# Experts in float16 halves, with the first layer's units on the partitions

## The chip, the cores and the metric

One core of a Trainium2 chip. The metric is device time in microseconds (us) of one launch; "the span" is the time from the first to the last instruction in the profile, and the device time of the same execution is 1.8 us longer.

## The reference

Hashed attention over 4 batches of 8 heads (768 tokens, 64 numbers a head), then a mixture layer with one expert per batch, applied to the 128 tokens of the batch with the highest gate scores:

```python
mask = q_bucket[:, :, :, None] == k_bucket[:, :, None, :]
scores = np.where(mask, scale * np.matmul(q, k.transpose(0, 1, 3, 2)), -1e9)
attn = softmax(scores)                      # max, exp, sum
x = attn @ v                                # heads side by side: 512 numbers a token
...
scores = np.einsum('bsd,d->bs', x, w_gate)
for b in range(B):
    top_idx = np.argpartition(-scores[b], capacity)[:capacity]
    xe = x[b, top_idx]                      # 128 x 512
    h = np.maximum(xe @ w1, 0.0)            # 128 x 1024
    ye = h @ w2                             # 128 x 512
    g = 1.0 / (1.0 + np.exp(-scores[b, top_idx]))
    out[b, top_idx] = x[b, top_idx] + g[:, None] * ye
```

## The kernel before

The 32 heads follow each other as a software pipeline. For each head a maximum phase (products mx, L340) runs some 14 units ahead of its score products (st, L385 and L389), the exponentials on ScalarE (L403, L405), the subtraction R on VectorE or GpSimd (L418), which gives the low half of the exponentials, and the attention products (av, L442). Where a number has to be kept to float32, it is held as a high and a low half and the product is made of three products.

The order of all this is written out by hand: every step has a time in units (nine to a head) worked out from the table T, a heap hands the steps out in order of time, and each engine gets its instructions in that order and keeps it. The token choice and the expert of a batch are generators in the same heap: what a generator yields is how many units later it goes on. `load_w` splits the two weight matrices into halves in the first 11 heads or so: a copy on ScalarE (L508) and a subtraction on GpSimd (L510), 16 of each.

Batch 0's expert is applied by `apply_expert` after the choice of batch 0, between heads 12 and 15. Batch 1's expert runs late, after batch 2's choice (the first `yield` below), mixed into heads 28 to 31 (heads are counted from 0); when it ends, batch 2's begins, no earlier than the second `yield` says:

```python
        if b == 2:
            yield -(9 * (NH - 2) + T["m1"])
            for y in apply_expert(1):
                yield y * T["y1"]
            yield -(9 * NH + T["m2"])
            st["fast"] = apply_expert_fast(2, LATE, mo_bank, mx_bank)
            yield from st["fast"]
```

A negative yield is an absolute time (here 253.1 and 279.3), and the choice and pause ahead of expert 1 end at 258.2, so that it starts there. Batch 3's part is the end of the kernel: `rank_last` takes the last scores (a product, a sum and two small steps on VectorE, after the last reciprocal L454 and its six copies on ScalarE L467), spreads them over the partitions by TensorE (bp, L851), compares on VectorE (L528 to L536), counts on TensorE (L540), finds the indices (idx, L882) and gathers the 128 rows (xe, L606). Then whatever expert 2 has not yet issued is issued, then eight products that only keep TensorE at work (wp, L894), then expert 3 (`apply_expert_last`).

An expert goes so: four transposes (xp, L628), three halves of xe (L635 to L637), the first layer of 24 products of 512 columns in two halves (mh, L662), a relu (L668), eight transposes (ht, L674), three halves of h (L686, L687, L692), the second layer of 24 products of 512 columns (yp, L700), the gate (L644 to L654), one step on VectorE that adds the result to the row (ye, L707) and a scatter by GpSimd's queue (L708).

Of the kernel before, what the change touches and what calls it, by code (L numbers as in the profile page):

```python
# [21 lines left out]
P = 128  # L22
# [9 lines left out]
VS = 16.0  # L32
DS = 2.0 ** -60
# [7 lines left out]
XHB = 2  # L41
# [10 lines left out]
    f2=2.4, l0=2.78, l1=6.42, l2=0.65, l3=5.3, lw=0.16, lw1=4.2, lw2=3.2, po=7.32,  # L52
# [30 lines left out]
def body(ctx, tc, qk, v, pj, wg, w1, w2, cst, out):  # L83
# [68 lines left out]
    w1h = cp.tile([P, 4, FF], F32R, name="w1h")  # L152
    w1l = cp.tile([P, 4, FF], BF16, name="w1l")
    w2h = cp.tile([P, 8, DM], F32R, name="w2h")
# [339 lines left out]
    def load_w(i):  # L494
# [11 lines left out]
        for e in range(2):  # L506
            sl = slice(e * 512, e * 512 + 512)
            nc.scalar.copy(hi[:, sl], t[:, sl])  # L508
            yield 1
            turn(nc.gpsimd.tensor_tensor(  # L510
                lo[:, sl], t[:, sl], hi[:, sl].bitcast(F32), op=ALU.subtract
            ))
            yield T["lw2"]
# [98 lines left out]
    def expert(b, tags):  # L612
# [19 lines left out]
        def split_x():  # L632
            xp = t["xp"]
            xh, xl, xb = tile_("xth", 512, F32R), tile_("xtl", 512, F32R), tile_("xtb", 512, BF16)
            nc.scalar.copy(xh, xp)  # L635
            nc.vector.tensor_tensor(xl, xp, xh.bitcast(F32), op=ALU.subtract)
            nc.scalar.copy(xb, xh.bitcast(F32))  # L637
            t["x"] = ((xh, w1h), (xl, w1h), (xb, w1l))
            t["hs"] = tile_("hs", FF, F32)
# [11 lines left out]
        def gate2():  # L651
            ss = t["ss"]
            nc.vector.tensor_scalar(ss[:, 1:2], ss[:, 1:2], 1.0, None, op0=ALU.add)
            nc.vector.reciprocal(ss[:, 1:2], ss[:, 1:2])  # L654

        def up(hp, e, ks, order=(0, 1, 2), by_part=False):
            ki = [(k, i) for k in ks for i in order]
            if by_part:
                ki = [(k, i) for i in order for k in ks]
            for k, i in ki:  # L660
                l, r = t["x"][i]
                nc.tensor.matmul(  # L662
                    hp, l[:, k * P : (k + 1) * P], r[:, k, e * 512 : e * 512 + 512],
                    start=(k == 0 and i == order[0]), stop=(k == 3 and i == order[-1]),
                )

        def relu(hp, e):
            nc.scalar.activation(t["hs"][:, e * 512 : e * 512 + 512], hp, AF.Relu)  # L668

        def turn_h(tp, e):  # L670
            t["tp", e] = tp
            for k in range(4):
                o = e * 512 + k * P
                nc.tensor.transpose(  # L674
                    out=tp[:, k * P : (k + 1) * P], in_=t["hs"][:, o : o + P], identity=ident
                )

        def split_h(e):
            if e == 0:
                t["h"] = [  # L680
                    (tile_("hth", FF, F32R), w2h), (tile_("htl", FF, F32R), w2h),
                    (tile_("htb", FF, BF16), w2l),
                ]
            (hh, _), (hl, _), (hb, _) = t["h"]
            f, tp = slice(e * 512, e * 512 + 512), t["tp", e]
            nc.scalar.copy(hh[:, f], tp)  # L686
            nc.scalar.copy(hb[:, f], hh[:, f].bitcast(F32))  # L687

        def split_h2(e):
            (hh, _), (hl, _), _ = t["h"]  # L690
            f, tp = slice(e * 512, e * 512 + 512), t["tp", e]
            nc.vector.tensor_tensor(hl[:, f], tp, hh[:, f].bitcast(F32), op=ALU.subtract)  # L692
# [20 lines left out]
        for f in (turn_x, split_x, gate, gate2, up, relu, turn_h, split_h, split_h2, down, finish):  # L713
# [4 lines left out]
        xth=("M3", 1), xtl=("M2x", 1), xtb=("M2", 2), hs=("M0", 1), hth=("M1", 1),  # L718
        htl=("M2x", 1), htb=("M3", 1), ye=("jk", 1),
    )  # L720
    LATE = dict(MAIN, htl=("X", XB), htb=("V", 1), ye=("X", XB))
    LAST = dict(
        xth=("XH", XHB), xtl=("XL", XLB), xtb=("R", 6), hs=("P", 4), hth=("P", 4),
        htl=("P", 4), htb=("P", 4), ye=("X", XB),
# [11 lines left out]
    def apply_expert(b):  # L736
# [9 lines left out]
        for e in range(2):  # L746
            hp = mo_bank(f"mh{b}_{e}")
            for k in range(4):
                m.up(hp, e, (k,))
                yield 1  # L750
            m.relu(hp, e)
            yield 2
        for e in range(2):
            m.turn_h(mo_bank(f"ht{b}_{e}"), e)
            yield 1
            m.split_h(e)
            yield 0.5
            m.split_h2(e)
            yield 1.5
# [7 lines left out]
    def apply_expert_fast(b, tags, bank, bank2):  # L767
# [7 lines left out]
        for k in range(4):  # L775
            m.up(h0, 0, (k,))
            yield T["f1"]
        m.relu(h0, 0)
        h1 = bank2(f"mh{b}_1")
        for k in range(2):  # L780
            m.up(h1, 1, (k,))
            yield T["f1"]
        m.gate2()
        m.turn_h(bank(f"ht{b}_0"), 0)
        m.split_h(0)
        yield T["f2"]
        m.split_h2(0)
        for k in range(2, 4):
            m.up(h1, 1, (k,))
            yield T["f1"]  # L790
        m.relu(h1, 1)
        yp = bank2(f"yp{b}")
        for k in range(2):
            m.down(yp, (k,))
            yield T["f1"]
        m.turn_h(bank(f"ht{b}_1"), 1)
        m.split_h(1)
        yield T["f2"]
        m.split_h2(1)
        for k in range(2, 8):  # L800
# [4 lines left out]
    def apply_expert_last(b, tags, bank, bank2):  # L805
# [6 lines left out]
        m.up(h0, 0, range(4), (0, 2, 1), True)  # L812
        m.relu(h0, 0)
# [238 lines left out]
```

## Time and profile before

| | |
|---|---|
| time, median of 3 runs (lowest to highest) | 487.26 us (485.84 to 487.91) |
| the profiled execution: time, span | 488.31 us, 486.5 us |
| mean granted TensorE clock | 0.956 |
| TensorE matmul busy | 430.6 us (89% of the span) |
| VectorE busy | 396.5 us (81%) |
| ScalarE busy | 344.0 us (71%) |
| GpSimd busy | 171.7 us (35%) |

The shares are means over stages that have different limits. The busy time of products is modelled and they overlap in the pipeline: one row's time is longer than the distance to the next, and what a product costs in a stream is the distance between starts.

### The profile page before, as it was taken

How to read it: one execution, taken by the hardware profiler on the slowest of the kernel's cores; microseconds unless marked ns; L12 is line 12 of the kernel's file. 1: busy time of each engine (PE TensorE's matmuls, PEld its weight loads, DVE VectorE, ACT ScalarE, POOL GpSimd, SP SyncE). 2: the span in 40 equal slices, each digit the busy share in tenths (PEclk: the TensorE clock that was granted, in tenths of full speed). 3: DMA queues.
4: the chain of work that ended last, by engine and by line, in shares of the span. 5: the costliest groups of instructions: out<-in, count | busy, mean ns of one | idle time of the engine just before them, and what ended most of it. 6: DMA issues, size and time to landing. Idle time of an engine off the chain costs nothing. (4 is left out here: it accounts for less than half of the span.)

```text
span 486.5 us, 14126 instructions
## 1 busy us (share of the span) xinstructions
PE 430.6 (89%) x5379; PEld 283.9 (58%) x5393; DVE 396.5 (81%) x991; ACT 344.0 (71%) x826; POOL 171.7 (35%) x137
## 2 busy tenths in 40 slices
PE   4789999978997898999998889899897899998795
PEld 3146666555654665676656566566565666666463
DVE  5669989999999997777799999999999977656611
ACT  2588898889885876787777579698775778763312
POOL 7025654445463352222413242324242333232300
PEclk9689999999999798999999899999998889999999
DMA  4774535545663233342464226445531133102010
GB/s 127 235 200 131 168 100 169 179 123 136 197 190 96 81 112 98 120 111 67 143 186 123 77 66 169 140 127 137 157 111 44 30 106 98 34 2 88 2 43 22
DMA packets 36167, 55.30 MB, mean 114 GB/s; under 512 B 6194, under 2 KB 27396, under 8 KB 36100
## 3 DMA queue, kind: packets, MB, share of 16 engines
q1 hardware_dynamic: 24676, 34.85, 26.2%
q10 hardware_dynamic: 10592, 17.44, 11.4%
q0 software_dynamic: 832, 2.11, 1.4%
q8 instruction: 42, 0.69, 0.6%
q14 instruction: 25, 0.20, 0.1%
HBM read 25.78 MB, written 7.35 MB: 68 GB/s over the span
## 5 line engine op out<-in xcount | busy, mean ns | idle before, releaser
L418 POOL TENSOR_TENSOR R<-P 128x768 f16<-128x768 f32 x80 | 124.9, 1562 | 246.9 <-DVE xd L334 95.1
L403 ACT ACTIVATE P<-st 128x512 f32<-128x512 f32 x192 | 113.2, 608 | 37.1 <-PE st L389 35.2
L442 PEld LDWEIGHTS <-P 128*128 128x128 bf16 x2304 | 120.1, 99 | 30.2 <-issue 20.3
L442 PE MATMUL av<-V,P 128*128 128x65 f16 (+1 forms) x2304 | 128.0, 196 | 0.0
L442 PE MATMUL av<-V,R 128*128 128x65 f16 x1152 | 123.1, 194 | 3.9 <-POOL R L418 2.3
L418 DVE TENSOR_TENSOR R<-P 128x768 f16<-128x768 f32 x112 | 119.5, 1067 | 7.0 <-ACT P L405 6.8
L385 PE MATMUL st<-A 97*128 97x256 f16 (+1 forms) x384 | 123.4, 333 | 0.3
L389 PE MATMUL st<-B 128*128 128x256 f16 (+1 forms) x384 | 123.3, 333 | 0.0
L356 DVE CUSTOM_DVE_ANT_0 mj<-mx,me 128x384 bf16<-128x384 f32 x192 | 106.2, 553 | 20.8 <-PE mx L340 8.4
L348 ACT ACTIVATE me<-mx 128x384 f32<-128x384 f32 x192 | 95.3, 497 | 28.7 <-DVE m L356 14.0
L442 PEld LDWEIGHTS <-R 128*128 128x128 f16 x1152 | 108.5, 100 | 5.2 <-POOL R L418 2.7
L340 PE MATMUL mx<-K,A 96*128 96x384 f16 x192 | 60.7, 344 | 10.4 <-DVE oneb L159 4.7
L405 ACT ACTIVATE P<-st 128x512 f32<-128x512 f32 x96 | 58.0, 604 | 11.3 <-PE st L389 10.0
L340 PE MATMUL mx<-A 96*128 96x384 f16 x192 | 64.6, 338 | 1.4 <-ACT me L348 0.7
L340 PEld LDWEIGHTS <-A 96*128 96x128 f16 x384 | 36.3, 100 | 30.0 <-issue 12.2
L467 ACT ACTIVATE x<-av,rc 128x64 f32<-128x64 f32 x192 | 42.2, 311 | 12.1 <-DVE rc L454 11.9
L385 PEld LDWEIGHTS <-A 97*128 97x128 f16 x384 | 38.1, 99 | 21.2 <-issue 7.2
L389 PEld LDWEIGHTS <-B 128*128 128x128 f16 x384 | 38.3, 100 | 18.7 <-issue 1.9
L235 DVE SCALAR_TENSOR_TENSOR XL<-X,XH 128x768 f16<-128x768 f32 x32 | 39.7, 1242 | 2.3 <-DMA B<-XL 2.3
L230 ACT ACTIVATE XH<-X 128x768 f16<-128x768 f32 x32 | 27.1, 850 | 7.6 <-DMA X<-in_qk_dram 7.6
L203 PE MATMUL hp<-X,pjt 128*32 128x384 f32 x128 | 17.6, 524 | 1.9 <-DMA X<-in_qk_dram 1.8
L334 DVE TENSOR_TENSOR xd<-XH 64x384 f16<-64x384 f16 x32 | 12.7, 397 | 8.0 <-ACT XH L230 7.1
(115 smaller groups left out, 498.4 us busy)
## 6 DMA issues: line engine op xcount, KB each, us to landing
X<-in_qk_dram SPq DMA_DIRECT2D x31, 384.0 KB
V<-in_v_dram ACTq DMA_DIRECT2D x16, 384.0 KB
A<-XH SPq DMA_DIRECT2D x64, 96.0 KB
B<-A SPq DMA_DIRECT2D x64, 96.0 KB
B<-XL SPq DMA_DIRECT2D x64, 96.0 KB
out_dram<-x ACTq DMA_DIRECT2D x8, 768.0 KB
W<-in_w_dram ACTq DMA_DIRECT2D x8, 512.0 KB
K<-xd SPq DMA_DIRECT2D x32, 48.0 KB
```

Source lines behind the costliest of these rows:

```text
L230: nc.scalar.activation(xh, st["X", h], AF.Copy, scale=XS)
L235: mine(nc.vector.scalar_tensor_tensor(xl, st["X", h], XS, st["XH", h], op0=ALU.mult, op1=ALU.subtract))
L340: nc.tensor.matmul(pt[:, :384], a[0:96, 0, t * P : (t + 1) * P], a[0:96, 1, 384:768] if i else K[h % NA][0:96], start=True, stop=True,)
L348: nc.scalar.activation(me, st["mx", h, t, 0][:, :384], AF.Relu)
L356: nc.vector.tensor_tensor_reduce(out=jk, in0=st["mx", h, t, 1][:, :384], in1=st["me", h, t], op0=ALU.add, op1=ALU.max, scale=1.0 / MS, sca ...
L385: nc.tensor.matmul(pt[:, o : o + n], a[:, 1, c * P : (c + 1) * P], a[:, 0, q0 : q0 + n], start=True, stop=False,)
L389: nc.tensor.matmul(pt[:, o : o + n], bt[:, 1, c * P : (c + 1) * P], bt[:, 0, q0 : q0 + n], start=False, stop=True,)
L403: nc.scalar.activation(pp[:, r, 0:512], pt, AF.Exp, scale=ES)
L405: nc.scalar.activation(pp[:, :, 512:768], pt.rearrange("p (a b) -> p a b", a=2), AF.Exp, scale=ES)
L418: (turn if pool else mine)(eng.tensor_tensor(t, pp[:, r, :], hi_view(pp, r), op=ALU.subtract))
L442: nc.tensor.matmul(o[:, t, 0:n], l, vv[:, c, hh, v0 : v0 + n], start=False, stop=last and l is lo, skip_group_check=True,)
L467: nc.scalar.activation(x[:, t], o[:, t, 0:D], AF.Copy, scale=rc[:, t : t + 1])
```

## The change

The high halves w1h and w2h, xth and hth become float16, and so do the low halves of x and h (the weights' low halves stay bfloat16). x is scaled by 16 on the way in, and the gate takes the 16 out again. The float16 high half serves in the third product too, so that the bfloat16 copies xtb and htb go. The first layer is turned round: the weights are the stationary operand and x the moving one, in 96 products of 128 columns instead of 24 of 512, so that the hidden units come out on the partitions. The second layer wants them there, and the transposes ht and the copy hs go; relu and split are made straight from the first layer's result, by ScalarE (high half) and VectorE (low half). The table T stays as it is, but for the entry f2, the two waits for a transpose in `apply_expert_fast`; the generators yield less in all, so that steps behind them get earlier times. The tiles that the halves use move to other tags.

```diff
-    w1h = cp.tile([P, 4, FF], F32R, name="w1h")
+    w1h = cp.tile([P, 4, FF], F16, name="w1h")
     w1l = cp.tile([P, 4, FF], BF16, name="w1l")
-    w2h = cp.tile([P, 8, DM], F32R, name="w2h")
+    w2h = cp.tile([P, 8, DM], F16, name="w2h")
...
             turn(nc.gpsimd.tensor_tensor(
-                lo[:, sl], t[:, sl], hi[:, sl].bitcast(F32), op=ALU.subtract
+                lo[:, sl], t[:, sl], hi[:, sl], op=ALU.subtract
             ))
...
-            xh, xl, xb = tile_("xth", 512, F32R), tile_("xtl", 512, F32R), tile_("xtb", 512, BF16)
-            nc.scalar.copy(xh, xp)
-            nc.vector.tensor_tensor(xl, xp, xh.bitcast(F32), op=ALU.subtract)
-            nc.scalar.copy(xb, xh.bitcast(F32))
-            t["x"] = ((xh, w1h), (xl, w1h), (xb, w1l))
-            t["hs"] = tile_("hs", FF, F32)
+            xh, xl = tile_("xth", 512, F16), tile_("xtl", 512, F16)
+            nc.scalar.activation(xh, xp, AF.Copy, scale=EX)
+            nc.vector.scalar_tensor_tensor(xl, xp, EX, xh, op0=ALU.mult, op1=ALU.subtract)
+            t["x"] = ((xh, w1h), (xl, w1h), (xh, w1l))
...
+        def up(hp, e, fs, order=(0, 1, 2)):
+            for i in order:
+                x, w = t["x"][i]
+                for f in fs:
+                    o = e * 512 + f * P
+                    for k in range(4):
+                        nc.tensor.matmul(
+                            hp[:, f * P : (f + 1) * P], w[:, k, o : o + P],
+                            x[:, k * P : (k + 1) * P],
+                            start=(f == 0 and k == 0 and i == order[0]),
+                            stop=(k == 3 and i == order[-1]), skip_group_check=True,
+                        )
+
+        def split_h(hp, e):
             if e == 0:
...
+                hh, hl = tile_("hth", FF, F16), tile_("htl", FF, F16)
+                t["h"] = ((hh, w2h), (hl, w2h), (hh, w2l))
             (hh, _), (hl, _), _ = t["h"]
...
+            f = slice(e * 512, e * 512 + 512)
+            nc.scalar.activation(hh[:, f], hp, AF.Relu)
+            nc.vector.scalar_tensor_tensor(
+                hl[:, f], hp, 0.0, hh[:, f], op0=ALU.max, op1=ALU.subtract
+            )
...
     MAIN = dict(
-        xth=("M3", 1), xtl=("M2x", 1), xtb=("M2", 2), hs=("M0", 1), hth=("M1", 1),
-        htl=("M2x", 1), htb=("M3", 1), ye=("jk", 1),
+        xth=("M3", 1), xtl=("M2x", 1), hth=("M1", 1), htl=("M0", 1), ye=("jk", 1),
     )
...
         for e in range(2):
             hp = mo_bank(f"mh{b}_{e}")
-            for k in range(4):
-                m.up(hp, e, (k,))
+            for f in range(4):
+                m.up(hp, e, (f,))
                 yield 1
-            m.relu(hp, e)
-            yield 2
-        for e in range(2):
-            m.turn_h(mo_bank(f"ht{b}_{e}"), e)
-            yield 1
-            m.split_h(e)
-            yield 0.5
-            m.split_h2(e)
-            yield 1.5
+            m.split_h(hp, e)
+            yield 0.5 + e
         yp = mo_bank(f"yp{b}")
...
-        for k in range(4):
-            m.up(h0, 0, (k,))
+        for f in range(4):
+            m.up(h0, 0, (f,))
             yield T["f1"]
-        m.relu(h0, 0)
+        m.split_h(h0, 0)
         h1 = bank2(f"mh{b}_1")
-        for k in range(2):
-            m.up(h1, 1, (k,))
+        for f in range(4):
+            m.up(h1, 1, (f,))
             yield T["f1"]
+        m.split_h(h1, 1)
         m.gate2()
-        m.turn_h(bank(f"ht{b}_0"), 0)
-        m.split_h(0)
-        yield T["f2"]
-        m.split_h2(0)
-        for k in range(2, 4):
-            m.up(h1, 1, (k,))
-            yield T["f1"]
-        m.relu(h1, 1)
         yp = bank2(f"yp{b}")
-        for k in range(2):
-            m.down(yp, (k,))
-            yield T["f1"]
-        m.turn_h(bank(f"ht{b}_1"), 1)
-        m.split_h(1)
-        yield T["f2"]
-        m.split_h2(1)
-        for k in range(2, 8):
+        for k in range(8):
             m.down(yp, (k,))
             yield T["f1"]
         m.finish(yp)
...
-        m.up(h0, 0, range(4), (0, 2, 1), True)
-        m.relu(h0, 0)
-        m.up(h1, 1, range(2), (0, 2, 1), True)
-        m.turn_h(bank(f"ht{b}_0"), 0)
-        m.split_h(0)
-        m.split_h2(0)
-        m.up(h1, 1, range(2, 4), (0, 2, 1), True)
-        m.relu(h1, 1)
+        m.up(h0, 0, range(4), (0, 2, 1))
+        m.split_h(h0, 0)
+        m.up(h1, 1, range(4), (0, 2, 1))
+        m.split_h(h1, 1)
         m.gate2()
         yp = bank2(f"yp{b}")
-        m.down(yp, range(2), (0, 2, 1), True)
-        m.turn_h(bank(f"ht{b}_1"), 1)
-        m.split_h(1)
-        m.split_h2(1)
-        m.down(yp, range(2, 4), (0, 2, 1), True)
+        m.down(yp, range(4), (0, 2, 1), True)
         m.down(yp, range(4, 8), (0, 2, 1), True)
```

## Rows read from the trace of the kernel before

**Rows 1.** Stretches of 10 us: their length, busy us (and instructions) by engine, clock, DMA.

```profile
260.00:270.00 10.00, 7.45 (x103) 5.20 (x101) 9.60 (x26) 5.31 (x12) 2.02 (x1) 1.00 0.40 107
...
410.00:420.00 10.00, 9.87 (x106) 6.66 (x108) 6.22 (x16) 7.11 (x20) 2.94 (x2) 1.00 0.16 41
```

**Rows 2.** Timeline of VectorE: the reciprocals of heads 21 and 23.

```profile
319.77 0.19 DVE L454 RECIPROCAL rc<-rc 128x6 f32<-128x6 f32 x1
...
340.60 0.19 DVE L454 RECIPROCAL rc<-rc 128x6 f32<-128x6 f32 x1
```

**Rows 3.** Timeline of TensorE: around a step of expert 1's first layer.

```profile
406.94 0.38 PE L385 MATMUL st<-A 97*128 97x512 f16 x1
407.15 0.38 PE L389 MATMUL st<-B 128*128 128x512 f16 x1
...
408.07 0.33 PE L340 MATMUL mx<-K,A 96*128 96x384 f16 x1
```

**Rows 4.** Timeline of TensorE: first and last of 12 products of a V sum.

```profile
418.60 0.22 PE L297 MATMUL sp<-V,ones 128*128 128x130 f16 x1
...
419.24 0.22 PE L301 MATMUL sp<-V,ones 128*128 128x128 f16 x1
```

**Rows 5.** Groups by line and shape: busy us, mean ns, idle before.

```profile
L297 PEld LDWEIGHTS <-ones 128*128 128x128 f16 x96 | 9.6, 100 | 7.6 <-issue 5.9
...
L687 ACT CAST htb<-hth 128x512 bf16<-128x512 f32 x8 | 4.9, 618 | 0.3
L674 PE MATMUL ht<-cs,hs 128*128 128x128 f32 x32 | 4.8, 273 | 0.0
...
L707 DVE SCALAR_TENSOR_TENSOR ye<-yp,ss,xe 128x512 f32<-128x512 f32 x4 | 3.0, 748 | 7.9 <-PE yp L700 7.9
```

**Rows 6.** Timelines of the engines at the end: start, length, engine, instruction, idle before.

```profile
444.00 0.20 PE L442 MATMUL av<-V,R 128*128 128x65 f16 x1 [0.61 <-DVE R L418]
...
444.48 0.19 PE L442 MATMUL av<-V,R 128*128 128x65 f16 x1
...
444.71 0.17 DVE L452 TENSOR_SCALAR rc<-av 128x6 f32<-128x6 f32 x1 [0.76 <-PE av L442]
...
448.36 1.60 PE L851 MATMUL bp<-cs,sc 128*128 128x128 f32 x12 [0.83 <-DVE ss L653]
449.72 0.48 PE L662 MATMUL mh<-w1h,xth 128*128 128x512 f32 x1
...
452.46 0.69 DVE L692 TENSOR_TENSOR htl<-ht,hth 128x512 fp32r<-128x512 f32 x1 [3.89 <-ACT hth L686]
453.06 0.87 DVE L528 TENSOR_SCALAR_CACHE_REDUCE cm<-sbc,sc 128x640 bf16<-128x640 f32 x1
...
460.86 1.05 POOL L606 DMA_INDIRECT xe<-out_dram,idx  x1 [7.46 <-DVE idx L882]
...
465.91 2.21 PE L894 MATMUL wp<-w1h 128*128 128x512 f32 x8
...
467.73 0.59 PEld L628 LDWEIGHTS xp<-cs,xe 128*128 128x128 f32 x4
467.96 0.60 PE L628 MATMUL xp<-cs,xe 128*128 128x128 f32 x4
```

**Rows 7.** DMA issues from 440 us on: median us to landing.

```profile
xe<-out_dram,idx POOLq DMA_INDIRECT x1, 3.4
```

**Rows 8.** Instructions of L510 and L418: ns min/median/max, first and last start.

```profile
L510 POOL TENSOR_TENSOR w1l<-W,w1h x8: 1266/1566/1994, 35.4 to 87.6; 128x512 bf16<-128x512 f32 x8
...
L418 DVE TENSOR_TENSOR R<-P x112: 946/955/2241, 29.5 to 443.0; 128x768 f16<-128x768 f32 x112
L418 POOL TENSOR_TENSOR R<-P x80: 1462/1468/2188, 31.4 to 441.1; 128x768 f16<-128x768 f32 x80
```

**Rows 9.** Stretches of 1 us, columns as in rows 1: the granted clock.

```profile
461.00:462.00 1.00, 1.00 (x4) 0.52 (x2) 0.17 (x1) 0.00 (x0) 0.91 (x1) 0.50 0.00 0
...
464.00:465.00 1.00, 1.00 (x6) 0.60 (x4) 0.00 (x0) 0.00 (x0) 0.00 (x0) 0.93 0.00 0
```

More of the change, by code (lines that the diff above doesn't have):

```diff
@@ L32 @@
 VS = 16.0
+EX = 16.0
 DS = 2.0 ** -60
@@ L51 @@
     norm=0.5, sc=0.14, scd=2.39, m1=-16.89, m2=-8.68, y1=1.0, sc3=0.31, f0=4.81, f1=0.93,
-    f2=2.4, l0=2.78, l1=6.42, l2=0.65, l3=5.3, lw=0.16, lw1=4.2, lw2=3.2, po=7.32,
+    l0=2.78, l1=6.42, l2=0.65, l3=5.3, lw=0.16, lw1=4.2, lw2=3.2, po=7.32,
     mo=0.58, ym=1, ch=3.2, ct=1.5, h23=5.59, cy=2.0, ml=1.08, xw=6.0,
@@ L652, in gate2 @@
             ss = t["ss"]
-            nc.vector.tensor_scalar(ss[:, 1:2], ss[:, 1:2], 1.0, None, op0=ALU.add)
+            nc.vector.tensor_scalar(ss[:, 1:2], ss[:, 1:2], 1.0, EX, op0=ALU.add, op1=ALU.mult)
             nc.vector.reciprocal(ss[:, 1:2], ss[:, 1:2])
[L656 to L671, printed above, removed]
-            for k in range(4):
[L673 to L678, printed above, removed]
-            if e == 0:
[L680 to L687, printed above, removed]
@@ L689, in split_h2 @@
-        def split_h2(e):
-            (hh, _), (hl, _), _ = t["h"]
-            f, tp = slice(e * 512, e * 512 + 512), t["tp", e]
-            nc.vector.tensor_tensor(hl[:, f], tp, hh[:, f].bitcast(F32), op=ALU.subtract)
+        def up(hp, e, fs, order=(0, 1, 2)):
[10 more added lines that the diff above has]
+                        )
@@ L711, in finish @@
             )
-        for f in (turn_x, split_x, gate, gate2, up, relu, turn_h, split_h, split_h2, down, finish):
+        for f in (turn_x, split_x, gate, gate2, up, split_h, down, finish):
             setattr(m, f.__name__, f)
@@ L717, in body @@
     MAIN = dict(
-        xth=("M3", 1), xtl=("M2x", 1), xtb=("M2", 2), hs=("M0", 1), hth=("M1", 1),
-        htl=("M2x", 1), htb=("M3", 1), ye=("jk", 1),
+        xth=("M3", 1), xtl=("M2x", 1), hth=("M1", 1), htl=("M0", 1), ye=("jk", 1),
     )
-    LATE = dict(MAIN, htl=("X", XB), htb=("V", 1), ye=("X", XB))
+    LATE = dict(MAIN, ye=("X", XB))
     LAST = dict(
-        xth=("XH", XHB), xtl=("XL", XLB), xtb=("R", 6), hs=("P", 4), hth=("P", 4),
-        htl=("P", 4), htb=("P", 4), ye=("X", XB),
+        xth=("XH", XHB), xtl=("XL", XLB), hth=("P", 4), htl=("P", 4), ye=("X", XB),
     )
@@ L774, in apply_expert_fast @@
         h0 = bank(f"mh{b}_0")
-        for k in range(4):
-            m.up(h0, 0, (k,))
+        for f in range(4):
+            m.up(h0, 0, (f,))
             yield T["f1"]
-        m.relu(h0, 0)
+        m.split_h(h0, 0)
         h1 = bank2(f"mh{b}_1")
-        for k in range(2):
-            m.up(h1, 1, (k,))
+        for f in range(4):
+            m.up(h1, 1, (f,))
             yield T["f1"]
+        m.split_h(h1, 1)
         m.gate2()
-        m.turn_h(bank(f"ht{b}_0"), 0)
-        m.split_h(0)
-        yield T["f2"]
-        m.split_h2(0)
-        for k in range(2, 4):
-            m.up(h1, 1, (k,))
-            yield T["f1"]
-        m.relu(h1, 1)
-        yp = bank2(f"yp{b}")
-        for k in range(2):
-            m.down(yp, (k,))
-            yield T["f1"]
-        m.turn_h(bank(f"ht{b}_1"), 1)
-        m.split_h(1)
-        yield T["f2"]
-        m.split_h2(1)
-        for k in range(2, 8):
+        yp = bank2(f"yp{b}")
+        for k in range(8):
             m.down(yp, (k,))
```

## The prediction

> **What bounds the kernel now.** I read the stretches of 10 us first, since the change touches only the four experts. Where an expert is mixed into the heads, TensorE is busy 9.87 of 10 us while VectorE has 6.2 and ScalarE 7.1; in the stretch of a token choice it is the other way round, VectorE 9.60 and TensorE 7.45 [rows 1]. Heads with neither take 10.4 us each: the reciprocals of heads 21 and 23 are 20.83 apart [rows 2]. So work taken from TensorE comes back where experts run, work taken from VectorE where they don't, and removed ScalarE work comes back nowhere: all 20 of its copies that go (xtb, hs and htb, five an expert, 0.62 us each or a little less [rows 5]) stand where it waits for TensorE. Were ScalarE the full engine there, they would give 3 us an expert.
>
> Then the timeline of the end. I call E the start of the last attention product, 444.48 [rows 6]. From there to the start of the last expert (xp, 467.73) are 23.25 us, and from there to the end of the span (486.5) 18.8. Two things in these 23.25 us aren't the ranking's own work. VectorE stands 3.89 us ahead of htl (452.46), a copy of expert 2 that lies in its queue before the ranking's first comparison (453.06). And the gather, issued at 460.86, lands 3.4 us later [rows 7], at about 464.3, while TensorE still has expert 2's second layer and the eight warm-up products to do and reaches xp only at 467.73.
>
> **The change part by part.** *TensorE work of an expert.* A step of the old first layer (three products of 512 columns) costs 0.70: from the st product at 407.15 to the next mx at 408.07 is 0.92, less the 0.22 of the st product itself (407.15 less 406.94) [rows 3]. The second layer has the same three forms, 0.70 too. The new step is 12 float16 products of 128 columns. The nearest rows are the 12 products of the V sum, 128 and 130 columns of float16 behind 128x128 weight loads: 418.60 to 419.24 for 11 of them, 58 ns each [rows 4]. So a step is 0.69 and the first layer keeps its cost, 5.5. The second layer goes to three 512-column float16 products, 0.215 each as the st pair stands: 0.65 a step, -0.4 in eight. The eight transposes go: one alone shows 0.27 [rows 5] and four in a row, those of xp, 0.60 from the first start to the last end [rows 6], so 0.11 from start to start and -0.9 for eight. Together -1.3 an expert.
>
> A page of the Trainium skill speaks against the shape: "TensorE: Matmul & The Clock Gate", section "Back-to-back issue gap", has streams of weight load and product at about 81 ns for 128 columns. By it, a first layer would take 7.8 us. The trace's 58 ns disagrees with it, if only for one weight tile loaded again and again; it is a rival below.
>
> *Expert 0*, in heads 12 to 15: -1.3 by TensorE. Bounds 0 (the heads' other engines set the pace in the freed time) and -1.6; I take -1.2, as TensorE is the full engine there.
>
> *Expert 1 and 2, the order.* The written order isn't edited, but its times follow from the yields. Expert 1 yields 22 units where it yielded 30, and expert 2 starts when expert 1 ends, so at 280.19 instead of 288.19. Its first layer then lies at 285.0 to 292.4, ahead of the last two attention products (290.75 and 291.91), where it lay behind them at 293.0; its second layer at 292.44 to 298.95, ahead of or around the ranking's broadcast (296.33), and its result (finish, 299.88) ahead of the comparisons (302.75). Into the full TensorE before E come 8 steps, +5.5; out go expert 1's -1.3; the two waits of TensorE for R before the last attention products (0.61 as shown [rows 6] and one like it of 0.38) are filled, -1.0. E moves by +3.2. Bounds +2.0 (the heads' other gaps fill too) and +4.2 (nothing is filled).
>
> *From E to xp.* Expert 2's last hidden half is now relu'd and split just before the last reciprocal in VectorE's queue. The first layer ends 0.84 before E (27 attention products of 31 ns; 16 of them start from 444.00 to 444.48), ScalarE needs 0.3 until it sees it and 0.6, VectorE 0.75 for its part (the same operation from PSUM takes 748 ns, ye [rows 5]; 0.69 as a subtraction, htl; hidden everywhere but here) and 0.33 for the gate: it comes free for the reciprocal at E+1.1, where it began at E+0.23. So the scores are late by 0.85, the broadcast bp starts at E+4.7 instead of 3.88. Five second-layer steps (3.2) stand before bp and are over by then; three (1.95) stand behind its 1.36. That is E+8.0; then the drain, and finish occupies VectorE from 8.2 to 8.95. Only then the comparisons begin, at E+8.95 against 453.06, E+8.58. So htl's stall is gone but finish takes its place, and nothing is won there: +0.4. From there to the gather's issue is the same 7.8, plus 0.3 for small products at the low clock: E+17.0. The gather lands 3.4 later, and xp starts at E+20.6, as nothing is left on TensorE but the warm-up: 8 products, 1.8 us at the high clock and 3.5 at half, done by E+19.9. So -2.6 against 23.25. Bounds -1.2 (finish waits longer for TensorE) and -3.6 (finish lands before the comparisons are ready). Moved with it are both scatters on GpSimd's queue, 1.0 us each: the first now stands before a subtraction of head 31, which it can make late by that much at most (E's upper bound covers it); the second is issued some 7 us before the gather behind it. No DMA of SP's queue moves.
>
> *The last expert:* the same -1.3, all of it on the path, since TensorE has work through both copies (hidden half 0 is copied during the 2.75 us of half 1, half 1 during the 2.6 of the first second-layer half). Bounds -1.0 (a copy shows) and -2.2 (before, a transposed half had to be copied twice between the layers, and some of that showed).
>
> *Weight loading, heads 0 to 11.* GpSimd subtracts a float16 now where it read a 4-byte float, 16 times 1.27 us at least. Its other subtraction reads 2-byte seconds and takes 1.46 for 768, 0.97 for 512: 16 x 0.3 = 4.7 us less. VectorE's R takes 0.95 alone and up to 2.24 [rows 8], and these heads are VectorE's. Bounds 0 and -2.5; I take -1.0, as most of GpSimd's time there is other work.
>
> *The clock.* From E+8 to E+16 TensorE has only counts of one column. After the like of it before, the clock had fallen to half (granted 0.50 in 461 to 462), and it was back in 464 to 465 (0.93), when the dense products of expert 2 had run on for a while [rows 9]. Now the warm-up is those dense products, ending as xp starts. I take 0; the other bound is a last expert that begins at half and stays there as long as those rows, some 3.4 us, half of it lost: 1.7.
>
> *Sum:* -1.2 + 3.2 - 2.6 - 1.3 - 1.0 = -2.9. The profiled execution is 488.31 (486.5 of span and 1.8 around it): 485.4. The median of the runs is 1.05 below it, so **484.4**.
>
> **The rivals.** First, *the forecast*: 484.4, own range 482 to 486, chance 0.50. For it: each term stands on rows; against it: it is a difference of terms larger than itself.
>
> Second, *the clock*: the last expert begins at half, +1.7: 486.1, chance 0.18. For it: expert 2 no longer fills the time of the gather; against it: the warm-up does for 3.5 us.
>
> Third, *nothing comes back in the heads*: neither expert 0 nor the subtractions return time, +2.2: 486.6, chance 0.16. For it: heads with no expert are held by VectorE and TensorE alike; against it: 9.87 of 10.
>
> Fourth, slower: *weight loads set the pace of the small products*. Every product of the first layer now brings new weights, and a load is busy 100 ns [rows 5]. If loads didn't overlap each other, a first layer would be 9.6, +4.1 for each of four, 500.8. It decides from (2.9 + 2.4) / 384, that is from 14 ns over the 58, 72 ns: there the kernel is 0.5% slower. Against it: loads of attention follow each other within 31 ns. By the 81 ns of the page of the Trainium skill named above it would be +8.8, 493.2. Chance 0.08, since the V sum's weights never change.
>
> Fifth, *the early first layer costs all of its time*: E moves by 4.2 and the reciprocal and finish wait longer, -1.2 in place of -2.6, +2.4: 486.8, with the clock 488.5. Chance 0.08.
>
> **Chances.** About 0.5% (2.4 us) is what a measurement can tell from no change: faster is below 484.8, slower above 489.7. The forecast is faster in two thirds of its cases and a better subtraction adds some; the second, third and fifth are mostly the same; the fourth and tails of the second and fifth are slower. Faster 0.44, same 0.41, slower 0.15. The range 480.9 to 488.4 holds all but the fourth and the best ends.
>
> **What would show it.** First-layer products 58 ns apart, or 72 and more. The reciprocals of heads 12 to 15 in about 1.2 less. The last attention product some 1 us later than before (3.2 less 1.2 and 1.0), no wait for R before it. Finish of expert 2 ahead of the comparisons, VectorE idle before it. xp about 20.6 after E, directly on the gather's landing. Granted clock 1.00 from xp on, or 0.50. A kernel that is faster by 6 would mean that the heads gave back more than TensorE's own share; one that isn't faster, that E moved by over 5.

## The result and the profile after

The changed kernel takes 480.73 us (median of 4 runs, 480.22 to 481.58), the kernel before 486.55 (4 runs, 485.34 to 487.91). The ratio used here and below is that of the runs in the fast state, 0.9893 with a 95% interval of 0.9847 to 0.9938; the two medians alone give 0.9880. It is faster by more than the 0.5%, as the largest of the three chances (0.44) had it. Against the 487.26 that the prediction started from, its range is 0.987 to 1.002 and holds the ratio; in microseconds, 480.73 lies 0.17 below the range's lower end. The forecast of 484.4 was 3.7 us too slow, and its own range of 482 to 486 was missed: the gain is about twice the one forecast. The profiled execution has a span of 479.1 us and a mean granted clock of 0.974.

The views are read in the order of the prediction. First the stretches between the marks it uses. The windows of after begin at the reciprocals of heads 0, 11, 15, 26 and 27, at the last attention product (E), and at xp's first product; the last ends with the span. Columns as in [rows 1].

```profile
44.59:182.62 138.03, 123.31 (x1742) 82.99 (x1737) 130.19 (x304) 113.27 (x279) 65.75 (x44) 0.98 0.51 144
182.62:238.61 55.99, 54.00 (x752) 37.37 (x751) 44.17 (x111) 41.76 (x101) 16.13 (x12) 1.00 0.40 115
238.61:378.24 139.63, 124.90 (x1769) 84.49 (x1769) 132.25 (x340) 107.86 (x268) 43.10 (x29) 0.98 0.43 118
378.24:391.63 13.39, 12.24 (x160) 8.43 (x158) 11.29 (x29) 8.21 (x21) 6.79 (x5) 0.87 0.36 98
391.63:441.84 50.21, 50.21 (x782) 38.51 (x781) 34.45 (x86) 31.73 (x80) 15.24 (x11) 1.00 0.13 40
441.84:461.92 20.08, 12.70 (x79) 6.23 (x75) 10.38 (x40) 2.29 (x8) 5.20 (x8) 0.83 0.19 66
461.92:479.10 17.18, 11.32 (x124) 8.06 (x124) 3.66 (x8) 1.99 (x4) 0.98 (x1) 0.97 0.04 16
```

The same lengths for every profile, in us (each is the difference of two starts in its timeline, as above):

| kernel | heads 1-11 | 12-15 | 16-26 | 27 | to E | E to compare | E to xp | xp to end |
|---|---|---|---|---|---|---|---|---|
| before | 139.47 | 58.72 | 139.60 | 14.99 | 47.92 | 8.58 | 23.48 | 18.54 |
| before2 | 139.36 | 56.60 | 139.67 | 12.03 | 47.91 | 8.57 | 24.74 | 18.61 |
| after | 138.03 | 55.99 | 139.63 | 13.39 | 50.21 | 8.78 | 20.08 | 17.18 |
| after2 | 138.23 | 55.10 | 141.19 | 12.03 | 50.21 | 8.78 | 20.10 | 17.19 |
| f16_only | 137.63 | 55.17 | 140.98 | 12.03 | 46.97 | 8.48 | 22.96 | 17.87 |
| late_expert2 | 138.03 | 57.64 | 141.36 | 14.98 | 48.72 | 9.74 | 21.10 | 18.76 |
| late_expert2b | 139.23 | 55.55 | 144.38 | 12.02 | 48.27 | 9.71 | 21.08 | 17.19 |
| late_finish | 140.74 | 54.24 | 141.18 | 12.02 | 50.20 | 6.68 | 18.33 | 19.23 |
| late_finish_warm | 139.35 | 54.52 | 141.20 | 12.03 | 50.21 | 6.68 | 18.33 | 18.86 |
| no_warm | 139.27 | 56.00 | 141.05 | 12.03 | 50.21 | 8.79 | 20.06 | 19.66 |
| best1 | 138.00 | 55.64 | 143.92 | 12.03 | 51.73 | 6.05 | 17.70 | 17.44 |
| best3 | 138.05 | 55.55 | 139.66 | 12.03 | 48.27 | 6.65 | 19.92 | 18.85 |
| f32_sub | 139.24 | 54.18 | 141.24 | 12.02 | 50.21 | 8.79 | 20.06 | 17.20 |
| f32_sub2 | 140.19 | 55.63 | 139.82 | 12.03 | 50.21 | 8.78 | 20.06 | 17.16 |

Between the two first profiles the span falls by 7.4: -1.44 in heads 1 to 11, -2.73 in 12 to 15, -1.60 in head 27, +2.29 to E, -3.40 from E to xp, -1.36 behind it, and +0.84 ahead of and in heads 0 and 16 to 26. Not all of it is the change's. Head 27 takes 12.02 or 12.03 in eleven of the fourteen profiles; in before, after and late_expert2 it holds a stretch at half clock (its mean is 0.87 in after).

The timelines of after at the end, the rows that answer to [rows 6]:

```profile
441.84 0.19 PE L443 MATMUL av<-V,R 128*128 128x65 f16 x1
441.87 0.38 PE L685 MATMUL yp<-w2h,hth 128*128 128x512 f16 x1
...
446.37 1.60 PE L805 MATMUL bp<-cs,sc 128*128 128x128 f32 x12 [1.10 <-DVE sc L796]
...
457.81 3.38 PE L848 MATMUL wp<-w1h 128*128 128x512 f16 x8
461.92 0.63 PE L629 MATMUL xp<-cs,xe 128*128 128x128 f32 x4 [0.73 <-DMA xe<-out_dram,idx]
463.23 1.05 PE L661 MATMUL mh<-xth,w1h 128*128 128x128 f16 x16 [0.69 <-ACT xth L636]
464.12 1.06 PE L661 MATMUL mh<-xth,w1l 128*128 128x128 f16 x16
...
441.87 0.69 DVE L675 SCALAR_TENSOR_TENSOR htl<-mh,hth 128x512 f16<-128x512 f32 x1 [1.36 <-ACT hth L674]
...
443.12 0.19 DVE L455 RECIPROCAL rc<-rc 128x6 f32<-128x6 f32 x1
...
449.95 0.75 DVE L692 SCALAR_TENSOR_TENSOR ye<-yp,ss,xe 128x512 f32<-128x512 f32 x1 [3.64 <-PE yp L685]
450.62 0.87 DVE L529 TENSOR_SCALAR_CACHE_REDUCE cm<-sbc,sc 128x640 bf16<-128x640 f32 x1
...
458.42 1.00 POOL L607 DMA_INDIRECT xe<-out_dram,idx  x1 [5.62 <-DVE idx L836]
```

The first-layer products stand 0.89 us for 16 apart (463.23 to 464.12): 55.6 ns each, each with weights of its own. So a step is 0.67, and the price that the prediction took from the V sum [rows 4] was right. The page "TensorE: Matmul & The Clock Gate" of the Trainium skill, section "Back-to-back issue gap", has 81 ns for such a stream; the trace disagrees, and it decides. (The same section has about 56 ns for a product alone, and that is what is seen.) htl of expert 2 lies just ahead of the reciprocal (443.12, E+1.28), bp follows at E+4.53, and the place where htl stalled VectorE before is taken by finish: VectorE sits 3.64 us until TensorE is through expert 2's second layer, and compares at 450.62, right behind it. xp begins on the gather's landing, TensorE having been idle 0.73.

The clock there, in stretches of 1 us of after, which answer to [rows 9]:

```profile
455.00:456.00 1.00, 0.32 (x5) 0.24 (x5) 0.96 (x5) 0.00 (x0) 0.00 (x0) 0.50 0.00 0
460.00:461.00 1.00, 1.00 (x4) 0.20 (x2) 0.00 (x0) 0.00 (x0) 0.00 (x0) 0.57 0.70 176
461.00:462.00 1.00, 0.27 (x2) 0.12 (x2) 0.00 (x0) 0.00 (x0) 0.00 (x0) 1.00 0.22 86
```

It falls to half (1.2 GHz) while TensorE has only counts, and it is back (2.4 GHz) in the warm-up's last product, about 1 us ahead of xp.

### The profile page after: what moved, and what is told of

It reads as the page before. It is cut to its first block, busy times and chain, and to the rows that moved or that the text cites. A ratio compares the mean times of both kernels' runs of the same rounds, so it can differ in the third digit from the quotient of the medians.

```text
span 479.1 us, 14641 instructions
## 1 busy us (share of the span) xinstructions
PE 424.2 (89%) x5649; PEld 283.3 (59%) x5649; DVE 395.8 (83%) x991; ACT 331.7 (69%) x806; POOL 169.5 (35%) x137
## 3 DMA queue, kind: packets, MB, share of 16 engines
q10 hardware_dynamic: 10592, 17.44, 11.8%
## 5 line engine op out<-in xcount | busy, mean ns | idle before, releaser
L443 PEld LDWEIGHTS <-P 128*128 128x128 bf16 x2304 | 118.9, 98 | 29.1 <-issue 19.0
L443 PE MATMUL av<-V,P 128*128 128x65 f16 (+1 forms) x2304 | 126.7, 196 | 0.0
L419 DVE TENSOR_TENSOR R<-P 128x768 f16<-128x768 f32 x112 | 118.0, 1055 | 9.1 <-ACT P L406 9.0
L204 PE MATMUL hp<-X,pjt 128*32 128x384 f32 x128 | 18.6, 540 | 2.1 <-DMA X<-in_qk_dram 2.1
```

The costliest lines, as they stand in the source:

```text
L419: (turn if pool else mine)(eng.tensor_tensor(t, pp[:, r, :], hi_view(pp, r), op=ALU.subtract))
L443: nc.tensor.matmul(o[:, t, 0:n], l, vv[:, c, hh, v0 : v0 + n], start=False, stop=last and l is lo, skip_group_check=True,)
```

## The experiments

The runs came in three groups, each with its own runs of the kernel before: 486.46 us (11 runs), 486.86 (16) and 485.99 (29).

**The two kernels again** (before2, after2: no edit).

> The kernel before, profiled a second time. Clock theory: part of what heads 12 to 15 and 27 gave back between the two profiles (2.7 and 1.6 us, where 1.2 and 0 were forecast) is only where the half-clock stretches happened to fall in the first profile (188 to 191 and 386 to 392 us); then in this profile head 11's to head 15's reciprocal is about 1.5 us under the 58.7 of the first, or the same stretches move elsewhere, and the time is 485 to 487. Shape theory: the old expert stretches themselves cost that much; then it is 58.7 again within 0.3.

> The changed kernel, profiled a second time. Clock theory: head 11 to head 15 moves off the 56.0 of the first profile by up to 1.7 either way with the half-clock stretches. Shape theory: 56.0 again within 0.3. Both: time 480 to 482.

Measured: 484.33 and 479.29 us, a run each. In the table, the marks of the end (to E, E to compare, xp to end) repeat to 0.07 (before2 has half clock between E and xp, hence 24.74), while heads 12 to 15 of before take 56.60 where they took 58.72, and heads 16 to 26 of after 141.19 where they took 139.63. Both differences lie at stretches of half clock that the other profile has elsewhere. In after2 the one in heads 16 to 26 is at 283 us, where after has none:

```profile
282.00:283.00 1.00, 1.00 (x8) 0.70 (x9) 1.00 (x5) 0.34 (x1) 0.00 (x0) 0.92 0.00 0
283.00:284.00 1.00, 1.00 (x11) 0.71 (x10) 1.00 (x2) 0.63 (x2) 0.00 (x0) 0.50 0.00 0
...
285.00:286.00 1.00, 1.00 (x9) 0.53 (x7) 0.26 (x1) 0.00 (x0) 0.75 (x1) 0.50 0.49 135
```

After has its own near 271 us instead, within a token choice, where VectorE is full (0.97 here; [rows 1] for the like of it in before):

```profile
270.00:271.00 1.00, 1.00 (x9) 0.60 (x7) 0.97 (x2) 1.00 (x3) 0.00 (x0) 0.50 0.07 18
```

Of the fourteen profiles, the five without a low stretch from 282 us to 320 us have 139.60 to 139.82 for heads 16 to 26, seven with one there 140.98 to 141.36, and two with more low clock in it 143.92 and 144.38. So the same fall of the clock costs nothing in a stage of VectorE's and about 1.5 us where TensorE is the full engine. Heads 1 to 11 show the like near 100 us: 139.23 to 139.35 in three profiles with a low stretch there, 138.00 to 138.23 in five of the same instructions without. late_finish, with 140.74, has that stretch and a second one at 175 to 179 us, and head 11 takes 13.56 there where it takes 11.98 in after:

```profile
176.00:177.00 1.00, 1.00 (x6) 0.75 (x5) 1.00 (x2) 0.42 (x1) 0.00 (x0) 0.50 0.00 0
```

Heads 12 to 15 move from profile to profile for another reason, since none of before2, after and after2 has half clock in them. TensorE waits there for the gather of expert 0's rows, and not equally long; the waits for it in before2, after and after2:

```profile
PE xp L628 <- DMA xe<-out_dram,idx: 1.1, 1, 1.1
```

```profile
PE xp L629 <- DMA xe<-out_dram,idx: 1.6, 1, 1.6
```

```profile
PE xp L629 <- DMA xe<-out_dram,idx: 0.7, 1, 0.7
```

Less this wait the heads take 55.5 in before2 and 54.4 in after and after2. (In late_finish, where the head before is late by its low clock, the wait is gone: 54.24.) So after and after2 differ there by the gather alone. Of the 2.1 between before and before2 the gather is 0.6 (the wait is 1.7 in before), and before's half clock at 187 to 191 us can be the rest. Neither theory had the gather.

**The float16 halves alone** (f16_only: the kernel before with the new types, the scale 16 and without xtb and htb; layout, transposes and yields stay).

```diff
+    w1h = cp.tile([P, 4, FF], F16, name="w1h")
...
+    w2h = cp.tile([P, 8, DM], F16, name="w2h")
...
+            nc.scalar.activation(xh, xp, AF.Copy, scale=EX)
...
+            t["x"] = ((xh, w1h), (xl, w1h), (xh, w1l))
...
+                t["h"] = ((hh, w2h), (hl, w2h), (hh, w2l))
...
-            nc.scalar.copy(hb[:, f], hh[:, f].bitcast(F32))
```

> The kernel before with the float16 halves alone: the first layer keeps its products of 512 columns, the relu'd copy, the transposes and all yields; the two bfloat16 copies go. Theory of the prediction (time is TensorE's products plus the subtractions of the weight loading): 1.4 off in heads 1 to 11, 0.5 to 0.8 off in each of experts 0, 1 and 3, about 3.0 in all, 483.5 or 0.994 of before. Rival (narrow halves are the whole gain and the layout nothing): 480.7, 0.988. Other rival (only the transposes and the order count): 486, 0.999.

Measured: 479.35 us (478.67 to 480.28, 4 runs), ratio 0.9852 (0.9802 to 0.9902). This part alone is as fast as the whole change, as far as the intervals can tell: the prediction's 0.994 lies outside them, the first rival's 0.988 inside. The windows of f16_only to E and to xp, and the timeline of TensorE ahead of xp:

```profile
390.30:437.27 46.97, 45.71 (x617) 31.04 (x621) 33.03 (x83) 31.13 (x79) 14.71 (x11) 1.00 0.14 42
437.27:460.23 22.96, 18.57 (x109) 9.10 (x108) 11.67 (x43) 4.65 (x13) 4.69 (x8) 0.93 0.17 58
```

```profile
458.50 1.89 PE L891 MATMUL wp<-w1h 128*128 128x512 f16 x8
460.23 0.60 PE L629 MATMUL xp<-cs,xe 128*128 128x128 f32 x4
```

E comes 0.95 earlier than in before, and xp still waits for TensorE's own queue, not for the gather (nothing idle ahead of 460.23). The whole change is 3.24 later at E, 2.88 shorter to xp and 0.69 shorter behind it: -0.33, which is nothing. So layout, missing transposes and the earlier expert 2 pay for each other. Stage by stage the halves give some 5.1 where the prediction had 3.0: 1.7 to 1.8 in heads 1 to 11, 1.2 in heads 12 to 15 (55.17, less 0.9 that TensorE stood before xp, against before2's 55.5), 0.95 to E, 0.5 from E to xp and 0.7 behind it. What the types and what the dropped copies xtb and htb give of it is not separated: no run has one without the other.

**Expert 2 at its old time** (late_expert2, and the same edit again, late_expert2b). A pause of 8 behind expert 1:

```diff
                 yield y * T["y1"]
+            yield 8
             yield -(9 * NH + T["m2"])
```

> The changed kernel with one more wait of 8 units behind expert 1, so that expert 2 starts at 288.19 as before. Theory of the prediction (expert 2's early first layer costs TensorE time before the last attention product E, and the stretch from E to xp has room for it): E 3.7 us earlier than in the changed kernel, E to xp some 0.9 longer (19.85 to about 20.7), 478 in all, 0.983 of before. Rival (its early start is what shortened E to xp): E 3.7 earlier, E to xp back near 23.2, so within 0.5 us of the changed kernel.

> The kernel with expert 2 at its old time, profiled again, because half-clock stretches lay at 382 to 389 and 440 to 443 us in its first profile. Theory: without them head 27's reciprocal to E is 46.5 to 47 (50.2 in the changed kernel) and E to xp about 21, 478. Rival: 48.7 as in the first profile.

Measured: 480.73 us (478.63 to 485.81, 9 runs), ratio 0.9890 (0.9856 to 0.9923), and 483.56 in the one run of the second. The stages are read from late_expert2b, since the profile of the first has half clock ahead of E. Its window to E and its waits of TensorE before that:

```profile
394.96:443.23 48.27, 45.47 (x683) 33.33 (x685) 33.26 (x83) 30.48 (x77) 15.21 (x11) 1.00 0.15 45
```

```profile
PE av L443 <- DVE R L419: 1.0, 1, 1.0
PE av L443 <- POOL R L419: 0.9, 1, 0.9
PE av L429 <- ACT x L468: 0.6, 1, 0.6
```

The early first layer costs 50.21 - 48.27 = 1.94 ahead of E, where 3.7 was expected, and brings 21.08 - 20.08 = 1.00 behind it, as expected: a loss of 0.9, too small for the times to show. Eight steps are 8 x 0.67 = 5.4; TensorE, idle for 48.27 - 45.47 = 2.80 without them, has no gap left with them (50.21 busy of 50.21), which accounts for 2.8 of the 3.4 that they don't cost. The second run's theory (46.5 to 47) failed too: without half clock E still comes at 48.27, no earlier than before's 47.92, though TensorE has 1.1 less to do. The two waits for R are 1.0 and 0.9 where they were 0.6 [rows 6] and 0.4. That expert 1 is over 8 units sooner may be why; no run tests it.

**Finish behind the comparisons** (late_finish), and the same with 4, 3, 2 and 2 extra products of 512 columns behind the first four counts, whose results nobody reads (late_finish_warm):

```diff
+        yield 8
         m.finish(yp)
...
+        wk = st_bank(f"wk{b}")
...
             count(i, cm, rp)
+            for _ in range((4, 3, 2, 2, 0, 0)[i]):
+                nc.tensor.matmul(wk, w1h[:, 0, 0:P], w1h[:, 0, 0:512], start=True, stop=True)
```

> The changed kernel with expert 2's last VectorE step put 8 units later, behind the ranking's comparisons. Theory of the prediction (that step stands in VectorE's queue where htl stood and holds the comparisons): the first comparison starts 2.1 us earlier after E (8.78 to about 6.7), 1.5 to 2.1 us faster than the changed kernel, 478.6 to 479.2. Rival (GpSimd's equalities or the broadcast hold the comparisons anyway): within 0.5 us of the changed kernel.

> The run with the late last step, with eleven extra products of 512 columns among the counts (their results are not used). Clock theory (that run won 1.75 us up to xp and lost 2.05 behind it because TensorE had too little to do while the ranking ran): the granted clock stays 1.00 from E to the end, E to xp 18.3, xp to the end 17.2 instead of 19.2, 478.5 to 479. Rival (the clock is not what made the last expert long): xp to the end stays at 19.

Measured: 480.26 us (477.81 to 481.52, 4 runs), ratio 0.9873 (0.9805 to 0.9941), and 479.91 (478.30 to 481.08, 10 runs), 0.9885 (0.9853 to 0.9918). In both the comparisons begin 2.10 earlier and xp 1.75 earlier, as they should if finish is what holds them; what they wait for in late_finish is the copy sbc of the broadcast:

```profile
448.72 0.88 DVE L529 TENSOR_SCALAR_CACHE_REDUCE cm<-sbc,sc 128x640 bf16<-128x640 f32 x1 [2.21 <-ACT sbc L811]
```

But the last expert takes 19.23 and 18.86 where it took 17.18. The timelines of TensorE, late_finish first, and a stretch of each:

```profile
456.17 3.58 PE L849 MATMUL wp<-w1h 128*128 128x512 f16 x8
460.37 1.09 PE L629 MATMUL xp<-cs,xe 128*128 128x128 f32 x4 [0.62 <-DMA xe<-out_dram,idx]
462.14 1.86 PE L661 MATMUL mh<-xth,w1h 128*128 128x128 f16 x16 [0.68 <-ACT xth L636]
```

```profile
461.00:462.00 1.00, 0.46 (x3) 0.19 (x2) 0.00 (x0) 0.51 (x1) 0.97 (x1) 0.50 0.08 16
```

```profile
454.74 1.89 PE L852 MATMUL wp<-w1h 128*128 128x512 f16 x8
458.94 0.63 PE L629 MATMUL xp<-cs,xe 128*128 128x128 f32 x4 [2.31 <-DMA xe<-out_dram,idx]
460.25 1.70 PE L661 MATMUL mh<-xth,w1h 128*128 128x128 f16 x16 [0.69 <-ACT xth L636]
461.75 1.91 PE L661 MATMUL mh<-xth,w1l 128*128 128x128 f16 x16
```

```profile
458.00:459.00 1.00, 0.07 (x1) 0.10 (x2) 0.00 (x0) 0.00 (x0) 0.00 (x0) 1.00 0.15 57
461.00:462.00 1.00, 1.00 (x12) 1.00 (x11) 0.53 (x2) 0.20 (x1) 0.00 (x0) 0.50 0.64 262
```

In late_finish the warm-up hasn't brought the clock back when xp begins, and 16 products take 1.66 (462.14 to the next 16 at 463.80) instead of 0.89. With the extra products the clock is up through the ranking, and the warm-up takes 1.89; then TensorE waits 2.31 for the gather, and the clock falls during the first layer. The gain of 1.75 at xp is lost behind it both times, once because the clock is not back in time and once because it falls again. That is read from one profile each; the medians say no more than that neither run is faster than the changed kernel by what can be told apart.

**No warm-up** (no_warm: `WARM = 0` for 8).

> The changed kernel without the eight warm-up products ahead of the last expert. Clock theory (the warm-up is what brings the clock back before xp): TensorE goes from the small products to xp with nothing dense between, the last expert starts at a granted clock of 0.50, and the time is 1.5 to 2.5 us longer, 482.3 to 483.2. Rival (the clock comes back by itself or the last expert does not hang on it): within 0.5 us of the changed kernel.

Measured: 483.01 us (480.33 to 485.36, 10 runs), ratio 0.9925 (0.9894 to 0.9956). Up to xp nothing changes; from xp to the end it takes 19.66, 2.48 more:

```profile
461.94 1.09 PE L629 MATMUL xp<-cs,xe 128*128 128x128 f32 x4 [3.95 <-DMA xe<-out_dram,idx]
463.71 1.86 PE L661 MATMUL mh<-xth,w1h 128*128 128x128 f16 x16 [0.69 <-ACT xth L636]
```

So the last expert of the changed kernel runs at the high clock because of the warm-up, as the term "clock 0" had it, and the second rival's price (1.7) was low: 2.5 by this run, 2.05 by late_finish, where the clock is back later than xp in spite of the warm-up.

**The subtraction.** f32_sub reads a 4-byte second operand again, but the same tile twice; f32_sub2 (the second diff) reads another tile:

```diff
-                lo[:, sl], t[:, sl], hi[:, sl], op=ALU.subtract
+                lo[:, sl], t[:, sl], t[:, sl], op=ALU.subtract
```

```diff
-                lo[:, sl], t[:, sl], hi[:, sl], op=ALU.subtract
+                lo[:, sl], t[:, sl], wgt, op=ALU.subtract
```

> The changed kernel, but GpSimd's subtraction in the weight loading reads a 4-byte float as its second operand again (the weight itself, so that the weights' low halves come out as zero). Theory (a 2-byte second operand makes the subtraction shorter, and VectorE gets the time back): the subtraction is 1.27 us at least as before, heads 1 to 11 take 1.4 us longer, 482.1. Rival (what heads 1 to 11 gave has another cause): they stay as in the changed kernel, 480.7.

> The changed kernel, but GpSimd's subtraction in the weight loading takes a separate tile of 4-byte floats as its second operand (the gate's weights, so that the weights' low halves are meaningless numbers). Theory (the 2-byte second operand gave heads 1 to 11 their 1.2 us): the subtraction takes 1.60 and 1.45 us again instead of 1.49 and 1.34, and heads 1 to 11 take 1.2 us longer, 139.4 instead of 138.1. Rival: the subtraction is longer and the heads are not.

Measured: 479.06 us (478.45 to 480.79, 4 runs), ratio 0.9843 (0.9795 to 0.9892), and 481.52 (478.87 to 485.60, 10 runs), 0.9933 (0.9891 to 0.9976). The instructions of the subtraction in after, with ns from shortest to longest, as in [rows 8], and then in f32_sub2:

```profile
L511 POOL TENSOR_TENSOR w1l<-W,w1h x8: 1154/1450/1882, 36.5 to 87.9; 128x512 bf16<-128x512 f32 x8
L511 POOL TENSOR_TENSOR w2l<-W,w2h x8: 1153/1160/1880, 102.0 to 162.8; 128x512 bf16<-128x512 f32 x8
```

```profile
L511 POOL TENSOR_TENSOR w1l<-W,wgt x8: 1267/1656/1998, 36.0 to 87.7; 128x512 bf16<-128x512 f32 x8
L511 POOL TENSOR_TENSOR w2l<-W,wgt x8: 1265/1279/1996, 102.4 to 164.7; 128x512 bf16<-128x512 f32 x8
```

f32_sub did not do what it was meant to: its means of 1395 and 1219 ns are shorter than after's 1484 and 1338. Its heads 1 to 11 take 139.24, with half clock at 99 to 103 and at 174 to 178 us; late_finish, with half clock at the same places and after's subtraction, takes 140.74. So a subtraction that is 1.7 shorter over all 16 goes with 1.5 less there. f32_sub2 has the lengths of before, and its heads 1 to 11 take 140.19, against 139.23 to 139.35 in the three that also have half clock near 100 us: 0.9 more, where 1.2 was expected. In both runs the subtraction also no longer reads ScalarE's copy, and so need not wait for it; that could be a part of f32_sub's gain, but not of f32_sub2's loss. So the shorter subtraction is worth about 0.9 there. The two ratios' intervals don't settle it; the stage does, by one profile each.

**Two versions meant to be best.** best1 is late_finish with expert 2 in between (the entry m2 at -5.3 for -8.68); best3 has expert 2 at its old time, splits the last half of h in its two parts, puts the low part and the last steps at written times behind the scores, and finish last:

```diff
-        yield T["f0"]
...
+        yield -292.0
...
-        m.split_h(h1, 1)
-        m.gate2()
+        m.split_hi(h1, 1)
...
+        yield -304.1
+        m.split_lo(h1, 1)
+        for k, t in ((4, 304.71), (5, 305.36), (6, 305.37), (7, 306.7)):
+            yield -t
+            m.down(yp, (k,))
+        yield -308
         m.finish(yp)
```

> The changed kernel with both waits mended by times alone: expert 2 starts at 282.7 units (its first layer mostly behind E, its splits in VectorE's gaps) and its last VectorE step comes 8 units later, behind the comparisons. Theory of the prediction: E 2.0 us earlier than in the changed kernel, E to xp 17.5 to 18 instead of 19.85, about 476.5, 0.979 of before. Rival (TensorE's work behind E now holds xp or the clock stays low for the last expert): 478.5 or more.

> The changed kernel with expert 2 placed by hand: start at 288.19 units, its first layer from 292.0 on, behind the last attention product E and around the broadcast, its second VectorE split between the comparisons, its second layer partly among the counts, its last step behind the ranking. Theory (the early expert 2 costs 3.3 us before E, its last step 2 us behind E, and TensorE that has products until the gather keeps its clock): E to head 27's reciprocal 46.5 to 47 instead of 50.2, E to xp 18.0 to 18.5 instead of 20.1, xp to the end 17.2; 475.5 where the changed kernel has 480.7, 0.978 of before. Rival (what is taken out before E comes back behind it): within 1 us of the changed kernel.

Measured: 482.20 us (478.42 to 483.12, 7 runs), ratio 0.9892 (0.9853 to 0.9932), and 480.69 (476.71 to 484.76, 12 runs), 0.9906 (0.9871 to 0.9941). best1 gains 2.38 from E to xp and loses 1.52 ahead of E, where it was to gain 2.0: TensorE waits 1.20 for the scaled x of a head and 1.93 for an R of GpSimd's. best3 has the early E (48.27) and the early comparisons (E+6.65), but xp at E+19.92, where 18.0 to 18.5 was expected. From the comparisons to the gather's issue it takes 9.69 instead of 7.80: the split stands between VectorE's comparisons, and VectorE waits for the last count, which stands behind expert 2's products on TensorE:

```profile
452.09 0.17 DVE L842 TENSOR_TENSOR rank<-rp,cnt 128x6 f32<-128x6 f32 x1 [1.13 <-PE rp L541]
```

Its last expert then takes 18.85, 1.67 more than after's, in a window with a clock of 0.83. Neither beats the changed kernel by what can be measured. The times are those of the rivals; best1's loss lies ahead of E, not behind it as its rival said.

## Why the prediction was right, and by how much off

*The sum.* The terms, each against what after's stages show beside before2's or before's, whichever has the clock up there (expert 0 less TensorE's wait for its gather; with it, -0.6 in after and -1.5 in after2):

| term | predicted | measured |
|---|---|---|
| weight loading, heads 1 to 11 | -1.0 | -1.1 to -1.4 |
| expert 0, heads 12 to 15 | -1.2 | -1.1 |
| E moves | +3.2 | +2.3 |
| E to xp | -2.6 | -3.4 |
| last expert | -1.3 | -1.4 |
| sum | -2.9 | -4.7 to -5.0 |

The medians differ by 5.8 (by the interval, 3.0 to 7.4), so the terms carry most of it; what the other 0.8 to 1.1 is, is not shown. All signs were right; the two that were mis-sized by most are E and E to xp, by 0.9 and 0.8, and both to the same side, so that the total is short by some 2 though no term is out by more than 0.9. What the stages don't confirm is the share of the layout in the heads: the prediction put 0.9 of an expert's 1.3 on the missing transposes, and f16_only, which keeps them, gives back as much in heads 12 to 15 and is at E sooner (46.97 against 48.27 in late_expert2b, whose expert 1 also runs earlier). The layout's own gains lie behind E: 1.88 from E to xp (late_expert2b's 21.08 against 22.96) and 0.69 behind it.

*"E moves by +3.2."* The step, put at 0.69, is 0.67, which is 0.16 for expert 2's eight and as much for expert 1's. The waits filled were put at the two that the timeline named, 1.0; TensorE's whole idle time from head 27 to E was 47.92 - 46.59 = 1.33 (before's window), and all of it is gone. These make some 0.65 of the 0.9; the rest stays open.

*"From E to xp 20.6."* The reciprocal was put at E+1.1 and came at 1.28; finish was put at 8.2 and came at 8.11, the comparisons at 8.78 for 8.95. That nothing is won up to the comparisons was right (+0.2). The loss of 0.3 at the low clock behind them didn't come: from the comparisons to the gather's issue are 7.80 in both. The issue is then at E+16.58 for 17.0, and xp 3.50 behind it. The 23.25 of before was counted to the start of xp's weight load and the 20.08 here to its first product; from product to product before has 23.48, so 0.2 of the 0.8 is that.

*"The last expert -1.3"* and *"-1.0 in weight loading"* stand: -1.36 in after, and about 0.9 by f32_sub2. Half of the last expert's gain comes with the halves alone (18.54 to 17.87 in f16_only).

*Expert 0* was right in size, -1.1 for -1.2, once TensorE's wait for the gather is taken out; the prediction had no such wait. The first two profiles show -2.73, of which before's stretch at half clock is a part: before2 has 56.60.

*The rivals.* The clock (second): fallen, by 1.00 in 461 to 462 and by no_warm, which shows what the other case costs. Nothing back in the heads (third): fallen. Weight loads (fourth): fallen, 55.6 ns where 72 decides. The early first layer costs all (fifth): fallen, it costs 1.94 of 5.4; but by late_expert2b it is a net loss of 0.9 (the prediction's own terms, +5.5 - 1.0 against -2.6, made it 1.9). What no rival had: the halves alone bring as much.

*What would show it* came: no wait for R before the last attention product, finish ahead of the comparisons with VectorE idle, xp on the gather's landing, the clock up from xp on (0.97 over the window, which falls only from 478 us on, when TensorE has nothing more to do). The sign for E did not come so plainly: against before it is 2.64 earlier in after (441.84 for 444.48) and 0.96 later in the second pair (440.21 for 439.25), which says more of the half clock in the stages ahead than of the change.

What stays open: which of the versions at 479 to 482 us is the fastest (their intervals overlap), whether the changed kernel draws fewer half-clock stretches than before (the profiles have 0.974 and 0.971 against 0.956 and 0.960, but those of the kernels built on it 0.947 to 0.978), and what the halves give without the dropped copies.

## What to carry to other kernels

Price a change in a mixed stage by the idle time of the engine that takes the work: eight steps of 5.4 us cost 1.9 where TensorE had 2.8 idle, and removed work brought nothing where the wait behind it was the longer. Where a change has several parts, time the smallest one alone: here new types, at a layout left as it was, gave as much as the whole. A gain in a stage that waits for a transfer is seen only when that wait is taken out. And look at the clock of the stage that follows before moving a start forward: 1.75 us won ahead of the last expert were lost in it, twice.

## What the runs showed of the hardware

- Stretches at half clock come at other places in each execution, in mid-kernel with TensorE busy too (1.00 of 1.00 at 283 to 284 in after2), and each costs nothing to about 1.5 us, by whether TensorE is the full engine there; the longer one in before's head 27 (385 to 393 us) cost 2.96 (14.99 - 12.03). That is the size of the effects looked for. The 29 runs of before spread from 481.03 to 489.36; how much of that is the clock's is not shown. The page "TensorE: Matmul & The Clock Gate" of the Trainium skill, section "What's actually happening", calls the slow phase of a kernel's start variable from run to run and puts its price under 1% of the span. No run here prices the start. The dearest single stretch in mid-kernel is under 1% too (2.96 of 486.5 is 0.6%), but so is what most of these runs were to tell apart.
- Weight loads of 128x128 float16, a new one for each product, don't set the pace: each is busy 98 ns, and the products stand 55.6 ns apart, no more than the 58 of the V sum, whose weights don't change [rows 4].

```profile
L661 PEld LDWEIGHTS <-w1h 128*128 128x128 f16 x256 | 16.1, 98 | 3.9 <-issue 0.9
```

- GpSimd's subtraction of 128x512 takes 1.27 us at least with a 4-byte second operand, 1.15 with a 2-byte one, and 1.04 (means 1.40 and 1.22) when both operands are one tile.
